# Sparse attention and a dropless mixture of experts on one core: expert work in units of up to 512 tokens instead of tiles of 128

## The chip, the core and the metric

The kernel runs on one core of a Trainium2 chip. Five engines work beside each other: TensorE (PE, with its weight loads shown as PEld), VectorE (DVE), ScalarE (ACT), GpSimd (POOL) and SyncE (SP), which issues most transfers. The metric is device microseconds (us) of one execution; lower is better.

## What is computed

The first half is block-sparse attention over 4 batches, 8 heads, 768 positions, head size 64. Its output is laid out as 3072 tokens of 512 numbers, and the second half sends each token through one of 8 experts:

```python
logits = x @ w_gate                      # (3072, 8)
expert_idx = np.argmax(logits, axis=1)
...
h = np.maximum(x_sorted[lo:hi] @ w1[e], 0.0)   # w1[e]: 512 x 1024
y_sorted[lo:hi] = h @ w2[e]                    # w2[e]: 1024 x 512
...
return (gate_w[:, None] * y).astype(np.float32)
```

All data are float32. With the reference's seed, experts 0 to 7 get 431, 32, 256, 32, 256, 160, 593 and 1312 tokens; of the first 2304 tokens (batches 0 to 2) they get 335, 32, 64, 32, 224, 128, 529 and 960. Neither kernel knows these counts when it is built: it counts on the chip, and has code for every case.

## The kernel before, in words

**Attention.** A loop over 16 pairs of heads and 2 halves computes scores, exponentials and sums, and writes token rows to a DRAM tensor `x_rows`, with each token's gate weight behind its 512 numbers. From the third batch on, routing work is put between.

**Routing, twice.** Phase A ranks the tokens of the first three batches while the last batch is still in attention, and gives `KA = 5` full tiles of 128 tokens to the experts that fill them. Phase B (`ranks`, `count`, `layout_b`, `one_hots`, `tokens`, lines 416 to 603) does it for the rest after attention. `tokens` makes lists of row numbers: `g` for gathers, `s` for scatters.

**Expert work, a tile at a time.** Each tile holds up to 128 tokens of one expert. `gather` (L620) is an indirect DMA issued by POOL. `fetch` (L629, L632) loads the expert's two weight matrices, 2 MB each, into one of two buffers. `turn_x` turns the rows so that features lie on partitions: by TensorE (L650) up to tile 5, by 16 DVE transposes (L642) later. `layer1` (L661) keeps blocks of w1 stationary and streams 128 tokens: 32 products, in fp32 two passes each, so 64 matmuls. `layer2` (L676) keeps the hidden values stationary and streams w2: 16 matmuls of 512 columns; its result has tokens on partitions, so that ACT scales it by the gate weight (L681) and POOL scatters it (L682) at once. Tiles share weight buffers in turn, and every tile fetches its own weights, the same expert's again too.

**Order.** On PE, DVE and POOL the instructions run as they are written down, between `by_hand.enter_context` and `by_hand.close()`; SP and ACT are ordered by the scheduler. 24 tiles are certain; a jump table (`tc.Switch`, L761) with one arm for each number of further tiles, 0 to 7, and a last arm that repeats everything in a safer way, closes the kernel. The counts above need 28 tiles, so arm 4 is taken. `judge` (L355) checks the attention's sums and decides whether the last arm is wanted.

Of the kernel before, what the change touches and what calls it, by code (L numbers as in the profile page):

```python
# [17 lines left out]
def kernel(  # L18
# [26 lines left out]
    NC = NT + E - 1  # L45
    TA = NT - NCH
    KA = 5
    NB_ = NC - KA
    assert TA * P - E * (P - 1) > (KA - 1) * P
# [32 lines left out]
    ld = ctx.enter_context(tc.tile_pool(name="ld", bufs=2))  # L82
# [4 lines left out]
    def load(b, pr):  # L87
        got = []
        for src, nm in ((k, "k_sb"), (q, "q_sb")):
            t = ld.tile([P, NCH, 2, D], F32, name=nm)  # L90
            for hh in range(2):

                queue = nc.scalar if nm == "q_sb" and (b, pr) == (0, 0) else nc.sync
                queue.dma_start(t[:, :, hh, :], src[b, 2 * pr + hh].rearrange("(p c) d -> p c d", p=P))
            got.append(t)
        t = ld.tile([P, 2, NCH, D], F32, name="v_sb", bufs=3)
        nc.sync.dma_start(
            t.rearrange("p h c d -> p h (c d)"), v[b, 2 * pr : 2 * pr + 2].rearrange("h (p c) d -> p h (c d)", p=P),
        )
        got.append(t)  # L100
        loaded[(b, pr)] = got
# [87 lines left out]
    def turn(b, pr, which):  # L189

        src = loaded[(b, pr)][which]
        dst = work.tile([P, S], F32, name="qT" if which else "kT")
# [15 lines left out]
    def scores(n, half, c):  # L208
# [11 lines left out]
        e = work.tile([P, 2, CW], F32, name="e", bufs=8)  # L220
        nc.scalar.activation(e[:], s[:, :, :CW], AF.Exp, scale=scale)  # L221
# [3 lines left out]
        if c > 0:  # L225
            t = esums[(n, half)]
            nc.vector.tensor_add(t[:], es[(n, half, 0)][:] if c == 1 else t[:], e[:])  # L227
# [80 lines left out]
    def shifted(n, half):  # L308
# [3 lines left out]
        for c in range(NCH):  # L312
            es[(n, half, c)] = work.tile([P, 2, CW], F32, name="e", bufs=8)
# [26 lines left out]
        for c in range(1, NCH):  # L340
            nc.vector.tensor_add(t[:], es[(n, half, 0)][:] if c == 1 else t[:], es[(n, half, c)][:])
# [13 lines left out]
    def judge():  # L355


        okp = ps_x.tile([1, 1], F32, name="okp", tag="xr")
        shape, total = [[4 * B * NPR, CW], [P, NT * E]], 0
        flats = (sums[:], lgn.rearrange("p t e -> p (t e)"))  # L360
        for j, (lo, hi) in enumerate(((2.0**-4, 2.0**40), (-(2.0**100), 2.0**100))):
            p, n = shape[j]
            total += p * n
# [5 lines left out]
            nc.tensor.matmul(okp[:], lhsT=okn[:], rhs=ones[:p, :1], start=(j == 0), stop=(j == 1))  # L369
        bad = mpool.tile([1, 1], F32, name="bad")  # L370
        nc.vector.tensor_scalar(bad[:], okp[:], scalar1=float(total), scalar2=float(REDO), op0=ALU.not_equal, op1=ALU.mult)

        nc.vector.tensor_scalar_min(rt["more"][:], rt["more"][:], float(NC - NT))
        arm = rt["arm"] = mpool.tile([1, 1], I32, name="arm")
        nc.vector.tensor_max(arm[:], rt["more"][:], bad[:])
# [4 lines left out]
    REDO = NC - NT + 1  # L380
# [8 lines left out]
    def route_consts():  # L389
        iota("first_w", [P, E], [[-1, E]], E, 0)  # L390
        iota("thr", [P, NT], [[P, NT]], 0, 0)
        iota("kx", [1, NC], [[1, NC]], 0, 0)
# [84 lines left out]
    def summed(out_, ph, off):  # L477

        r, sel = rt["r" + ph], rt["sel" + ph]
        T = r.shape[2]  # L480
        slot = sm.tile([P, E, T], F32, name="slot", tag="slot")
        nc.vector.tensor_tensor(slot[:], r[:], off[:].unsqueeze(2).to_broadcast([P, E, T]), op=ALU.add)
        nc.vector.tensor_tensor(slot[:], slot[:], sel[:], op=ALU.mult)
        nc.vector.reduce_sum(out_, slot.rearrange("p e t -> p t e"), axis=AX)
# [3 lines left out]
    def layout_a():  # L488
        cn = rt["cnA"]
        og = sm.tile([P, E, TA], F32, name="ogA")  # L490
        nc.vector.tensor_tensor(
            og[:], cn[:, 1, :].unsqueeze(2).to_broadcast([P, E, TA]), rt["thr"][:, None, 1 : TA + 1].to_broadcast([P, E, TA]),
# [7 lines left out]
        nc.vector.tensor_scalar_min(lo[:], lo[:], float(KA))  # L500
        nc.vector.tensor_scalar_min(hi[:], up[:], float(KA))
        nc.vector.tensor_sub(used[:], hi[:], lo[:])
        nc.vector.tensor_scalar(used[:], used[:], scalar1=float(P), scalar2=None, op0=ALU.mult)
        rt["used"] = used
        rt["lo"] = lo
        tile_experts("A", hi, KA)

    def slots_a():
        cn, r, lo, used = rt["cnA"], rt["rA"], rt["lo"], rt["used"]
        off = small_e("offA")  # L510
        nc.vector.scalar_tensor_tensor(off[:], in0=lo[:], scalar=float(P), in1=cn[:, 0, :], op0=ALU.mult, op1=ALU.add)
# [14 lines left out]
    def layout_b():  # L526
# [4 lines left out]
        og = sm.tile([P, E, NT], F32, name="ogB")  # L531
        nc.vector.tensor_tensor(
            og[:], left[:].unsqueeze(2).to_broadcast([P, E, NT]), rt["thr"][:, None, :].to_broadcast([P, E, NT]), op=ALU.is_gt,
        )
        nt, up = small_e("ntB"), small_e("upB")
        nc.vector.reduce_sum(nt[:], og[:], axis=AX)
        nc.vector.tensor_tensor_scan(up[:], nt[:], rt["zero"][:], 0.0, op0=ALU.add, op1=ALU.add)
        tile_experts("B", up, NB_)

        more_f = sm.tile([1, 1], F32, name="more_f")  # L540
        nc.vector.tensor_scalar(
            more_f[:], up[0:1, E - 1 : E], scalar1=float(KA - NT), scalar2=0.0, op0=ALU.add, op1=ALU.max,
        )
        rt["more"] = more_f
        base, off = small_e("base"), small_e("offB")
        nc.vector.tensor_sub(base[:], up[:], nt[:])
        nc.vector.scalar_tensor_tensor(base[:], in0=base[:], scalar=float(P), in1=used[:], op0=ALU.mult, op1=ALU.subtract)
        nc.vector.scalar_tensor_tensor(off[:], in0=base[:], scalar=-1.0, in1=cA[:, 0, :], op0=ALU.add, op1=ALU.add)
        sl = sm.tile([P, NT], F32, name="slB")
        summed(sl[:, :TA], "A", off)  # L550
# [3 lines left out]
        summed(sl[:, TA:], "B", off)  # L554
# [34 lines left out]
    def tokens(ph, T, n):  # L589
# [11 lines left out]
        nc.vector.tensor_scalar(none[:], tv[:], scalar1=0.0, scalar2=float(2 * N), op0=ALU.is_lt, op1=ALU.mult)  # L601
        s_ = kept("s" + ph, [P, n])
# [5 lines left out]
    st = [{} for _ in range(NC)]  # L608

    keep_w1 = [wp.tile([P, DB, F], F32, name=f"w1_{j}") for j in range(2)]  # L610
    keep_w2 = [wp.tile([P, FB, DM], F32, name=f"w2_{j}") for j in range(2)]
    keep_xg = [wp.tile([P, XW], F32, name=f"xg_{j}") for j in range(4)]
    keep_xT = [wp.tile([P, DB, P], F32, name=f"xgT_{j}") for j in range(2)]

    def of(name, i, p):
        return rt[name + "A"][:p, i : i + 1] if i < KA else rt[name + "B"][:p, i - KA : i - KA + 1]

    def gather(i):
        xg = st[i]["xg"] = keep_xg[i % 4]
        nc.gpsimd.indirect_dma_start(  # L620
            out=xg[:], out_offset=None, in_=x_d[: N - S, :] if i < KA else x_d[:, :], in_offset=bass.IndirectOffsetOnAxis(ap=of("g", i, P), axis=0),
        )

    def fetch(i, layer):

        e = nc.sync.value_load(of("xe", i, 1), min_val=0, max_val=E - 1)
        if layer == 1:
            w = st[i]["w1"] = keep_w1[i % 2]
            nc.sync.dma_start(w[:], w1v[:, bass.ds(e, 1)].rearrange("p e c f -> p (e c) f"))  # L629
        else:  # L630
            w = st[i]["w2"] = keep_w2[i % 2]
            nc.sync.dma_start(w[:], w2v[:, bass.ds(e, 1)].rearrange("p e a d -> p (e a) d"))  # L632

    def turn_x(i):
        xg, xT = st[i]["xg"], keep_xT[i % 2]
        st[i]["xT"] = xT
        if i > KA:

            for tq in range(4):
                for dq in range(4):  # L640
                    t, d = slice(tq * 32, (tq + 1) * 32), slice(dq * 32, (dq + 1) * 32)
                    nc.vector.transpose(xT[d, :, t], xg[t, :DM].rearrange("p (c q) -> p c q", c=DB)[:, :, d])  # L642
            return

        if i == 0 and "ps_m" not in upper:
            tp = upper["ps_s"].tile([P, 2, 512], F32, name="tp0", tag="s")[:, 0, :].rearrange("p (c q) -> p c q", c=DB)
        else:
            tp = upper["ps_m"].tile([P, DB, P], F32, name="tpg")[:]
        for c in range(DB):
            nc.tensor.transpose(tp[:, c, :], xg[:, c * P : (c + 1) * P], ident[:])  # L650
        nc.scalar.copy(xT[:], tp)

    def layer1(i, *between):

        hT = st[i]["hT"] = xp.tile([P, FB, P], F32, name="hT")
        for g in range(2):
            hp = upper["ps_h"].tile([P, FB // 2, P], F32, name="hp")
            for m in range(FB // 2):
                fb = g * (FB // 2) + m
                for c in range(DB):  # L660
                    nc.tensor.matmul(  # L661
                        hp[:, m, :], lhsT=st[i]["w1"][:, c, fb * P : (fb + 1) * P], rhs=st[i]["xT"][:, c, :],
                        start=(c == 0), stop=(c == DB - 1),
                    )
            if g == 0 and i >= KA:
                nc.vector.tensor_relu(hT[:, : FB // 2, :], hp[:])  # L666
            else:
                nc.scalar.activation(hT[:, g * (FB // 2) : (g + 1) * (FB // 2), :], hp[:], AF.Relu)  # L668
            if g == 0:
                for do in between:  # L670
                    do()

    def layer2(i, group):
        zp = upper["ps_z"].tile([P, DM], F32, name="zp")
        for fb in range(FB):
            nc.tensor.matmul(  # L676
                zp[:], lhsT=st[i]["hT"][:, fb, :], rhs=st[i]["w2"][:, fb, :], start=(fb == 0), stop=(fb == FB - 1),
            )
        zo = xp.tile([P, DM], F32, name="zo")
# [148 lines left out]
```

## Time and profile before

| what | value |
|---|---|
| three runs | 766.81, 767.39, 768.59 us; median 767.39 |
| profiled execution | 767.37 us, of which the span from first to last instruction is 765.7 |
| attention, to the first expert matmul | 0 to 357.5 us |
| 28 tiles | 357.5 to 754.8 us |
| PE, DVE, ACT, POOL busy | 749.5, 415.8, 270.2, 67.2 us |
| weights fetched | 56 transfers of 2 MB |

The page gives busy time by engine, then the span in 40 slices, then groups of instructions with their mean duration. The queries of the trace give single instructions in order of time, also those of an engine's sequencer (marked q: waits, branches, issues), which are not counted as busy.

### The profile page before, as it was taken

Reading aid. Unit: us, or ns where it says so; the run is one execution under the profiler, and the core shown is the slowest. Engines: PE = TensorE matmul, PEld = TensorE weight load, DVE = VectorE, ACT = ScalarE, POOL = GpSimd, SP = SyncE. Lnnn points to the kernel's source line nnn. Section 1 sums busy time; section 2 is a strip of 40 time slices with the busy share of each in tenths; the row PEclk is TensorE's granted clock in tenths of the full one; section 3 lists DMA queues with packets and bytes.
Section 4 is the critical chain, followed back from the end, with each engine's and each line's share of the span. In section 5 each row is a group of like instructions: output and inputs, shape, how many; then the busy total and the mean of one; then the engine's idle time right before and its main releaser. Section 6 shows DMA issues by size and latency. Waiting matters only on the chain.

```text
span 765.7 us, 13053 instructions
## 1 busy us (share of the span) xinstructions
PE 749.5 (98%) x5134; PEld 475.8 (62%) x5134; DVE 415.8 (54%) x834; ACT 270.2 (35%) x425; POOL 67.2 (9%) x98
## 2 busy tenths in 40 slices
PE   7999999999999999999999999999999999999994
PEld 4555555555555555556777686786776776866682
DVE  4678777777778779997530235533434425323400
ACT  4666676667666675665111000100100100001000
POOL 4000000000000000002011121111111211211010
PEclk8999999999999999999999999999999999999998
DMA  8322333233322331842789989899899899899940
GB/s 187 83 60 48 82 84 85 63 83 84 85 56 51 83 84 44 319 165 78 244 308 333 344 311 348 320 329 346 320 329 362 314 344 345 320 346 339 355 147 6
DMA packets 119362, 157.57 MB, mean 206 GB/s; under 512 B 56499, under 2 KB 72947, under 8 KB 119284
## 3 DMA queue, kind: packets, MB, share of 16 engines
q1 hardware_dynamic: 112672, 142.42, 55.8%
q0 software_dynamic: 4480, 13.75, 4.6%
q8 instruction: 43, 0.70, 0.4%
q10 hardware_dynamic: 2132, 0.41, 0.3%
q14 instruction: 35, 0.29, 0.1%
HBM read 143.79 MB, written 13.73 MB: 206 GB/s over the span
## 4 chain that ended last, share of the span: by engine, by line
PE 86%; DMA 7%; issue 5%; another core or an unknown queue 0%; ACTq 0%; POOL 0%; ACT 0%; DVE 0%; POOLq 0%
PE hp L661 21%; PE zp L676 19%; PE s L216 17%; PE op L237 16%; DMA out_dram<-zo,sB 6%; PE s L219 4%; PE sp L250 3%; PE xr L270 3%; PE tp L199 2%; DMA q_sb<-in_q_dram 1%; PE tpg L650 0%; POOL xg L620 0%; ACT qT L201 0%; ACTq L117 0%
## 5 line engine op out<-in xcount | busy, mean ns | idle before, releaser
L661 PEld LDWEIGHTS hp<-xgT,w 128*128 128x128 f32 x1792 | 204.7, 192 | 12.6 <-issue 8.6
L661 PE MATMUL hp<-xgT,w 128*128 128x128 f32 x1792 | 205.6, 275 | 0.0
L676 PE MATMUL zp<-w,hT 128*128 128x512 f32 x448 | 196.9, 593 | 0.0
L642 DVE STREAM_TRANSPOSE xgT<-xg 32x128 f32<-32x128 f32 x352 | 106.5, 303 | 110.0 <-DMA xg<-x_rows,gB 94.0
L216 PE MATMUL s<-qT,kT 64*128 64x384 f32 x768 | 159.2, 493 | 0.9 <-ACT qT L201 0.9
L221 ACT ACTIVATE e<-s 128x768 f32<-128x768 f32 x192 | 152.4, 812 | 7.0 <-PE s L219 5.2
L676 PEld LDWEIGHTS zp<-w,hT 128*128 128x128 f32 x448 | 83.0, 190 | 94.2 <-issue 94.2
L227 DVE TENSOR_TENSOR esum<-esum,e 128x768 f32<-128x768 f32 x128 | 122.7, 958 | 14.6 <-ACT e L221 1.1
L237 PE MATMUL op<-e,v_sb 128*64 128x384 f32 x768 | 129.3, 486 | 0.0
L237 PEld LDWEIGHTS op<-e,v_sb 128*64 128x64 f32 x768 | 55.1, 137 | 68.8 <-issue 68.8
L216 PEld LDWEIGHTS s<-qT,kT 64*128 64x128 f32 x768 | 67.1, 190 | 38.4 <-issue 33.5
L257 DVE RECIPROCAL r<-ss 128x128 f32<-128x128 f32 x96 | 82.2, 912 | 1.3 <-ACT ss L252 1.3
L668 ACT ACTIVATE hT<-hp 128x512 f32<-128x512 f32 x33 | 19.7, 597 | 177.4 <-PE hp L661 174.4
L681 ACT ACTIVATE zo<-zp,xg 128x512 f32<-128x512 f32 x28 | 19.2, 687 | 176.7 <-PE zp L676 176.7
L666 DVE TENSOR_SCALAR hT<-hp 128x512 f32<-128x512 f32 x23 | 15.9, 692 | 101.4 <-issue 57.9
L227 DVE TENSOR_TENSOR esum<-e 128x768 f32<-128x768 f32 x32 | 30.6, 957 | 63.2 <-ACT e L221 63.2
L219 PE MATMUL s<-pen,oh 64*128 64x384 bf16 x384 | 63.2, 326 | 0.0
L242 ACT COPY oT<-op 128x384 f32<-128x384 f32 x32 | 15.3, 479 | 106.2 <-PE op L237 106.2
L682 POOL DMA_INDIRECT out_dram<-zo,sB x23 | 23.3, 1013 | 259.7 <-ACT zo L681 259.7
L219 PEld LDWEIGHTS <-oh 64*128 64x128 bf16 x384 | 18.9, 95 | 25.8 <-issue 0.9
L270 PEld LDWEIGHTS xr<-mix,oT 128*64 128x64 f32 (+1 forms) x372 | 24.0, 139 | 10.7 <-issue 10.7
L250 PE MATMUL sp<-esum,ones 128*64 128x384 f32 x128 | 27.7, 512 | 0.0
(174 smaller groups left out, 260.1 us busy)
## 6 DMA issues: line engine op xcount, KB each, us to landing
w<-in_moe_w_dram SPq DMA_DIRECT2D x56, 2048.0 KB
k_sb<-in_k_dram SPq DMA_DIRECT2D x32, 192.0 KB
v_sb<-in_v_dram SPq DMA_DIRECT2D x16, 384.0 KB
x_rows<-xb SPq DMA_DIRECT2D x16, 384.0 KB
q_sb<-in_q_dram SPq DMA_DIRECT2D x30, 192.0 KB
sums<-ss SPq DMA_DIRECT2D x32, 3.0 KB
q_sb<-in_q_dram ACTq DMA_DIRECT2D x2, 192.0 KB
xg<-x_rows,gB POOLq DMA_INDIRECT x23, 7.5
```

Of the source, the lines that this page charges most:

```text
L216: nc.tensor.matmul(s[:, hh, :CW], lhsT=kT[r, c * P : (c + 1) * P], rhs=qT[r, cols], start=True, stop=False)
L219: nc.tensor.matmul(s[:, hh, :CW], lhsT=oh[r, c, :], rhs=pen[r, cols], start=False, stop=True)
L221: nc.scalar.activation(e[:], s[:, :, :CW], AF.Exp, scale=scale)
L227: nc.vector.tensor_add(t[:], es[(n, half, 0)][:] if c == 1 else t[:], e[:])
L237: nc.tensor.matmul(op[hh * D : (hh + 1) * D, :], lhsT=v_sb[:, hh, c, :], rhs=e[:, hh, :], start=(c == 0), stop=(c == NCH - 1),)
L250: nc.tensor.matmul(sp[hh * D : (hh + 1) * D, :], lhsT=ones[:], rhs=esum[:, hh, :], start=True, stop=True)
L257: nc.vector.reciprocal(r[:, m * P : (m + 1) * P], ss[:, m * P : (m + 1) * P])
L270: nc.tensor.matmul(xr[j * M_ : (j + 1) * M_, m, :], lhsT=oT[:, m * P + j * M_ : m * P + (j + 1) * M_], rhs=mix[:, pr, :], start=True, stop ...
L642: nc.vector.transpose(xT[d, :, t], xg[t, :DM].rearrange("p (c q) -> p c q", c=DB)[:, :, d])
L661: nc.tensor.matmul(hp[:, m, :], lhsT=st[i]["w1"][:, c, fb * P : (fb + 1) * P], rhs=st[i]["xT"][:, c, :], start=(c == 0), stop=(c == DB - 1),)
L676: nc.tensor.matmul(zp[:], lhsT=st[i]["hT"][:, fb, :], rhs=st[i]["w2"][:, fb, :], start=(fb == 0), stop=(fb == FB - 1),)
L682: ins = nc.gpsimd.indirect_dma_start(out=out[:, :], out_offset=bass.IndirectOffsetOnAxis(ap=of("s", i, P), axis=0), in_=zo[:], in_offset=N ...
```

## The change

Layer 2 is turned round: now w2 is stationary too (`lhsT=self.w2[...]`, 128x128 blocks), and the tokens stream in both layers, any number `n` of them up to 512. So a unit of n tokens is 64 + 64 matmuls, each n columns wide. The result of layer 2 has features on partitions; it has to be turned back before it is scaled and scattered. `finish` does this with 16 DVE transposes, then for each 128 tokens one POOL multiplication by the gate weights and one scatter.

There are three kinds of unit:

- `early`: 2 units of 256 tokens (phase A), turned by TensorE;
- `whole`: units of 384 tokens for experts with more than 512 left, 0 to 6 of them. The old end switch is now in the middle and has an arm for each number of whole units; the arm has the units and prepares unit `own[1]`;
- `own`: one unit for each expert, with what is left. Its gather, turn and finish always handle 4 x 128 tokens; the matmuls' width is 128 to 512 in steps of 16, chosen by a jump table of 25 arms on PE and ACT (on POOL too for the last). The last unit does layer 2 in the old way (`layer2_by_rows`).

With the counts above: 256 tokens each of experts 0 and 6 are early; expert 7 has 3 whole units; the own units' widths are 176, 128, 256, 128, 256, 160, 352, 160. Buffers of attention (`ar`, `ea`) are reused for the units' data. `hT` and `zo` exist once. `judge` moves ahead of `tokens("B")`, and the safer arm is followed by the normal own units whose scatters it turns off.

The core of the diff (left out: renamed buffers in attention, the changed constants of phase A, the safer arm):

```diff
+    EA, QA, UW, RW, GR = 2, 2 * P, 3 * P, 4 * P, 16
+    UM = -(-(N - EA * QA - RW) // UW)
...
+        if units:
+            ge = sm.tile(shape, F32, name="ge_u", tag="slot2")
+            nc.vector.tensor_tensor(ge[:], slot[:], wide(units[0]), op=ALU.is_ge)
+            nc.vector.tensor_tensor(ge[:], ge[:], wide(units[1]), op=ALU.mult)
+            nc.vector.tensor_tensor(slot[:], slot[:], ge[:], op=ALU.add)
...
+        def turn(self):
+            self.keep_gates()
+            for tq in range(4):
+                for dq in range(4):
+                    t, d = slice(tq * 32, (tq + 1) * 32), slice(dq * 32, (dq + 1) * 32)
+                    nc.vector.transpose(
+                        self.xT[d].rearrange("p c (j q t) -> p j c q t", j=RJ, q=4)[:, : self.nj, :, tq, :],
+                        self.xg[t, : self.nj, :DM].rearrange("p j (c q d) -> p j c q d", c=DB, q=4)[:, :, :, dq, :],
+                    )
...
+        def layer1(self, n, between={}):
+            for fb in range(FB):
+                hp = upper["banks"][fb % 6]
+                for c in range(DB):
+                    nc.tensor.matmul(
+                        hp[:, :n], lhsT=self.w1[:, c, fb * P : (fb + 1) * P], rhs=self.xT[:, c, :n],
+                        start=(c == 0), stop=(c == DB - 1),
+                    )
+                nc.scalar.activation(hT[:, fb, :n], hp[:, :n], AF.Relu)
+                for do in between.get(fb, []):
+                    do()
...
+        def finish(self, group):
+            for tq in range(4):
+                for dq in range(4):
+                    t, d = slice(tq * 32, (tq + 1) * 32), slice(dq * 32, (dq + 1) * 32)
+                    nc.vector.transpose(
+                        zo[t, : self.nj, :].rearrange("p j (c q d) -> p j c q d", c=DB, q=4)[:, :, :, dq, :],
+                        self.zT[d].rearrange("p c (j q t) -> p j c q t", j=RJ, q=4)[:, : self.nj, :, tq, :],
+                    )
+            for j in range(self.nj):
+                nc.gpsimd.tensor_scalar(
+                    zo[:, j, :], zo[:, j, :], scalar1=gates[:, self.at, j : j + 1], scalar2=None, op0=ALU.mult,
+                )
+                self.put(j, zo[:, j, :], group)
...
+    rows_out(n, 0)
+    early[0].layer1(QA, {2: [lambda: rows_out(n, 1)], 5: [turn_1], 7: [count_b]})
+    early[0].layer2(QA)
+    early[1].layer1(QA, {1: [tokens_b]})
+    whole(0, 0).fetch(2)
+    own[0].fetch(1)
+    early[1].layer2(QA)
+    own[0].fetch(2)
+    whole(0, 0).turn()
+    own[0].turn()
+    for u in early:
+        u.finish("rows_out")
...
+            units = [whole(i, arm - 1) for i in range(arm)]
+            for u, then in zip(units, units[1:] + [own[1]]):
+                then.gather()
+                u.layer1(UW)
+                then.turn()
+                then.fetch(1)
+                u.layer2(UW)
+                then.fetch(2)
+                u.finish("rows_out")
...
+    for e, u in enumerate(own):
+        if e + 2 < E:
+            own[e + 2].gather()
+        at = rt["size"][0:1, e : e + 1]
+        index = {
+            ET.PE: nc.tensor.value_load(at, min_val=0, max_val=(RW - P) // GR),
+            ET.Activation: nc.scalar.value_load(at, min_val=0, max_val=(RW - P) // GR),
+        }
+        if e + 1 == E:
+            index[ET.Pool] = nc.gpsimd.value_load(at, min_val=0, max_val=(RW - P) // GR)
+        for k in tc.Switch(index, (RW - P) // GR + 1):
+            width = P + k * GR
+            u.layer1(width)
+            if e + 1 < E:
+                u.layer2(width)
+            else:
+                u.layer2_by_rows(width, "rows_out")
+        if e + 2 < E:
+            own[e + 2].turn()
+            own[e + 2].fetch(1)
+            own[e + 2].fetch(2)
+        if e + 1 < E:
+            u.finish("rows_out")
```

PE, DVE and POOL follow the written order in the units too (`tc.manual_schedule`).

## The prediction

> **What bounds the kernel now.** I read the busy times and slices first, then the chain that ended last, then single instructions around the switch.
>
> ```profile
> PE 749.5 (98%) x5134; PEld 475.8 (62%) x5134; DVE 415.8 (54%) x834; ACT 270.2 (35%) x425; POOL 67.2 (9%) x98
> ...
> PE   7999999999999999999999999999999999999994
> ...
> DVE  4678777777778779997530235533434425323400
> ```
> ```profile
> 643.15 6.87 PE zp L676 x16
> 650.02 7.14 PE hp L661 x64
> 657.16 6.87 PE zp L676 x16
> ```
> The first fence (page) shows PE full in every slice and DVE at 2 to 5 tenths from slice 20 on. The second (chain) shows a tile as 7.14 + 6.87 = 14.01 us of PE with nothing between; no wait for weights appears, though they keep the DMA engines at 9 tenths. So only fewer matmul columns save time: the 56 fetches becoming 26 (13 units) saves nothing by itself. 28 tiles take 392.3 us.
>
> **Attention, phase A, first fetches.** Same instructions; up to 357.5 us I change nothing. Cover: PE, full there; without it one more x turn costs 0.6 us.
>
> **PE's matmuls.** A matmul of 128 columns takes 7.14/64 = 111.6 ns, of 512 columns 6.87/16 = 429.4 ns; a straight line gives 138 at 160, 151 at 176, 217.5 at 256, 297 at 352, 323.5 at 384. A unit is 128 of them: early 2 x 27.8, whole 3 x 41.4, own 19.4 + 14.3 + 27.8 + 14.3 + 27.8 + 17.7 + 38.0, the last 64 x 0.138 + 32 x 0.4294 = 22.6. Sum 361.7: **30.6 us less**.
>
> **Turning.** Now DVE turns into and out of each unit, 16 transposes each, of 512 elements in an own unit.
> ```profile
> 689.34 5.32 DVE L642 STREAM_TRANSPOSE xgT<-xg 32x128 f32<-32x128 f32 x16 [6.93 <-DMA xg<-x_rows,gB]
> ```
> ```profile
> L227 DVE TENSOR_TENSOR esum<-esum,e 128x768 f32<-128x768 f32 x128 | 122.7, 958 | 14.6 <-ACT e L221 1.1 <-DVE esum L227 0.5
> L642 DVE STREAM_TRANSPOSE xgT<-xg 32x128 f32<-32x128 f32 x352 | 106.5, 303 | 110.0 <-DMA xg<-x_rows,gB 94.0 <-PE hp L661 5.6
> ...
> L519 DVE TENSOR_TENSOR within<-rA,leftA 128x144 f32<-128x144 f32 x1 | 0.3, 309 | 0.0
> ```
> Timeline, then DVE's groups (busy, mean ns): one transpose of 128 elements takes 303 ns, 16 take 5.32 (29 ns between). Only one size is shown. Lower end: a fixed part and the slope of the additions, (958 - 309)/624 = 1.04 ns an element: 303 + 384 x 1.04 = 702 ns at 512. Upper end: all proportional, 1212 ns. I take 702, since the 144-element addition costs as much as the transpose, so the fixed part looks alike. With 29 ns and the copy of the gates, 16 take 11.9 us for 4 x 128 tokens (11.7 back), 9.8 for 384, 7.4 for 256; at the upper end 19.9. The Trainium skill ("Vector Engine (DVE) Microarchitecture Reference", 3.8) says that a transpose sustains one element a cycle and lane, which speaks for the lower end; by it the sum below is 866, by the upper end 1017.
>
> **POOL and its transfers.**
> ```profile
> L174 POOL COPY mix<-ident 128x128 f32<-128x128 f32 x4 | 1.2, 288 | 0.1
> L175 POOL COPY mix<-wg 128x8 f32<-128x8 f32 x4 | 0.8, 188 | 1.6 <-DMA wg<-in_moe_w_gate_dram 1.6
> ```
> ```profile
> 397.48 1.02 POOL L682 DMA_INDIRECT out_dram<-zo,sA  x1 [12.58 <-ACT zo L681]
> 398.80 0.97 POOL L620 DMA_INDIRECT xg<-x_rows,gB  x1 [0.30 <-issue]
> ```
> ```profile
> DMA to landing us min/median/max: 3.4/7.4/9.0
> ```
> POOL's groups: (288 - 188)/120 = 0.83 ns an element, so the multiplication of 512 is 0.61 us; from above I allow 1.2, twice that, as no tensor_scalar is shown. POOL's timeline: issues follow each other every 1.3 us. So a scaled scatter of 128 tokens is 1.9 us, a gather of an own unit 4 x 1.3 = 5.2. Third fence, the gathers (L620): landing 3.4 us after an issue starts on quiet queues, 7.4 under full weight traffic; that is 2.4 and 6.4 after POOL is free. I take 4.0, as weights will be half the traffic, and 2.5 for the first ones.
>
> **Jumps.**
> ```profile
> L761 PEldq TENSOR_LOAD <-arm x1: 487/487/487, 691.1 to 691.1; - x1
> L761 PEldq BRANCH_PREFETCH_HINT  x1: 50/50/50, 695.4 to 695.4; - x1
> L761 ACTq TENSOR_LOAD <-arm x1: 484/484/484, 699.0 to 699.0; - x1
> L761 POOLq TENSOR_LOAD <-arm x1: 511/511/511, 699.7 to 699.7; - x1
> ...
> L761 ACTq BRANCH_PREFETCH_HINT  x1: 57/57/57, 706.1 to 706.1; - x1
> L761 POOLq BRANCH_PREFETCH_HINT  x1: 69/69/69, 706.2 to 706.2; - x1
> ```
> The switch's line: from loading the arm's number to the first instruction of the arm PE needs 4.3 us, ACT 7.1, POOL 6.5. Here this cost nothing: PE's sequencer was 17 matmuls of 0.43 us ahead (the switch is read at 691.1, the matmuls before the arm run until 698.8). Leaving the arm: PE 0.4 (branch at 748.9, next at 749.2), ACT 2.4, POOL 2.9, SP 6.0. In front of an own unit PE is ahead by 17 matmuls of the unit before, 1.9 us (128 columns) to 5.5 (384). ACT can begin only when PE has ended the unit before: it is ready 0.25 + (0.4 to 6.0) + 0.75 + (2.5 to 6.0) later, middle 11.0, and PE can go on for six banks, 48 matmuls (5.4 us at 128). With 0.5 us for the first relu, own units lose 4.2 + 6.1 + 3.0 + 6.1 + 3.0 + 4.8 + 2.6 + 4.8 = **34.6 us** at the middle, about 7 with the shortest jumps. The skill ("Runtime: NRT & Kernel Launch", Instruction fetch mechanics) says that prefetch is sequential and a taken branch outside the window waits for a DMA; it gives no price, and PE's exit, far away and 0.4 us, does not show it.
>
> **Where it all goes: the ring.** DVE's written order is turn(e+2), finish(e); POOL's is gather(e+3) after the scatters of finish(e). So each own turn waits for a gather, that for scatters, these for a finish, that for the turn before. Walked through (span times):
>
> - Early. rows_out, layer 1, two turns: layer 1 of early 0 ends at 376.0, layer 2 at 389.9, PE reaches `tokens_b` at 393.4. DVE starts layout B at 376.2. It took 12.3 us (374.39 to 386.65); added: six wide operations 1.7, eight small 1.6, one-hots of 50 not 26 columns 1.8, smaller tables -1.0, and judge, now ahead, 2.9. PE waits and does its small products until 397.2: 3.8 us. Where this wait is gone, nothing else is late.
> - Early 1 goes on 24.4 to 421.5, jump 0.7, whole 0 41.4: to 463.7.
> - Beside it: gathers from 398.2, whole 0 turned 414.4, own 0 426.3, finish early 0 433.7, scatters 437.5, landing (`zo` exists once) 440.0, finish early 1 447.4, scatters 451.2, POOL's jump 457.7, gather whole 1 461.6, landed 465.6, turned 475.4. **PE waits 11.7 us.** Whole 1 ends at 516.8, whole 2 (turned 509) at 558.3.
> - Finish whole 2 568.5, scatters 574.2, POOL leaves the arm (2.9 and some five semaphore increments of 0.75 us) 581.2, gather own 2 586.4, landed 590.4, turned **602.3**. PE ends own 1 at about the same time.
> - One turn of the ring: 11.9 + 11.7 + 4 x 1.9 + 5.2 + 4.0 = **40.4 us**, against 22.7 us of PE per unit. Five rounds: own 7 is turned at 804.3.
> - End. Finish own 5 816.0, scatters 823.6, landed 827.6, finish own 6 839.3, scatters 846.9, POOL's jump 853.4, last scatters 855.7; 8.7 us follow (757.0 to 765.7 now): span 864.4. PE's last unit is done by 830.
>
> The profiled execution is 767.37 with a span of 765.7, 1.7 around; its time stands at the median of the runs (767.39). **Forecast 864.4 + 1.7 = 866 us.**
>
> Bounds of it: quick landings 2.4 make 853, slow ones 6.4 make 885; multiplications of 1.2 us make 887; all POOL and jump terms at their short end 838, several long ones 905. Transposes at the upper end make 1017.
>
> **Rivals.**
> - *The jumps bound, not the ring.* If DVE's and POOL's ring stays under PE's pace, the path is 546.5 (early and whole without the 11.7) + 181.9 + 34.6 + 10.6 tail + 1.7 = **775 us**. For it: DVE is half idle now; against: the written order.
> - *Faster.* The same with jumps at their short end: 546.5 + 181.9 + 7.3 + 10.6 + 1.7 = **748 us**. One mechanism: POOL's gathers do not stand behind the scatters, so that a unit's turning hides under two units of PE. It decides when a ring turn is below 22.7 us plus 3; with 40.4 the transposes would have to be free.
> - *Dearer transposes or POOL work*: over 905.
> - *It doesn't do what it says*: widths in the profile would be 512. The counts give widths that sum to 1616 columns, so I give this nothing beyond the rest.
>
> **Chances.** Ring, 838 to 905: 0.70. Jumps alone: 0.09. Faster: 0.10. Over 905: 0.08. Something between the two rivals within 0.2% of before: 0.03. A change under 0.2% can't be told from none here. The range for 8 in 10 takes in ring and jumps: 770 to 905; slower in all 0.87.
>
> **What would show it.** Right: DVE transposes of 512 elements near 0.70 us; PE waiting 10 to 25 us before own 3 to 7 for xT; POOL's gather right after the scatters; whole 1 late by some 12 us. Wrong: PE busy over 9 tenths in the last third, waits before own units under 6 us, or short waits that end with ACT's relu, which would mean the jumps.

## The result, and the profile after

| | before | after |
|---|---|---|
| median, us | 767.41 (four runs, 766.81 to 768.59) | 896.49 (four runs, 894.59 to 898.92) |
| ratio, 95% interval | 1 | 1.1681 (1.1649 to 1.1714) |
| span of the profiled execution | 765.7 | 895.4 |
| mean granted clock | 0.992 | 0.908 |

The change makes the kernel 16.8% slower. The forecast was 866 us, its range 770 to 905. The busy times and the slices of after (page; one digit is a fortieth of the span, 22.4 us):

```profile
PE 742.2 (83%) x4516; PEld 481.7 (54%) x4516; DVE 535.9 (60%) x858; ACT 288.8 (32%) x516; POOL 164.2 (18%) x175
...
PE   7999999999999999999977999865970757189820
...
DVE  4777787777777998478626443536272736363650
...
PEclk8999999999999999999998999976986797579875
```

For 20 slices (to 448 us) the line of PE looks as before. The two 7s after that are the wait before whole 1. From the 26th slice (560 us) on it has holes, and the clock falls with each hole. DVE's line now swings between 2 and 7 in a beat of two slices: a unit comes round every 44 us. PE's busy time fell by only 7.3 us although its columns are worth 30.6 us less, because after a wait the same matmuls run slower (own 2's 64 matmuls of 256 columns take 16.79 us in layer 1, after a wait, and 13.98 in layer 2).

The chain that ended last ran over PE before; now it runs over POOL (start, duration, what):

```profile
711.11 1.56 POOL ea L753
...
721.75 1.03 POOL out_dram L734
723.09 1.01 POOL ar L672
727.88 27.06 issue
```

Behind the "issue" of 27 us stand the landing of the gather and DVE's two turnings, which this view does not follow; the timelines do. One round of the beat, in the timelines of DVE, POOL and PE (start, duration, engine, line, what; in brackets the idle time before and what ended it):

```profile
731.64 0.17 DVE L689 COPY gates<-ar 128x4 f32<-128x4 f32 x1 [20.63 <-DMA ar<-x_rows,gB]
731.72 11.44 DVE L697 STREAM_TRANSPOSE xT<-ar 32x512 f32<-32x512 f32 x16
743.19 11.71 DVE L748 STREAM_TRANSPOSE ea<-ar 32x512 f32<-32x512 f32 x16
775.96 0.17 DVE L689 COPY gates<-xg 128x4 f32<-128x4 f32 x1 [21.06 <-DMA xg<-x_rows,gB]
```
```profile
755.00 1.56 POOL L753 TENSOR_SCALAR ea<-ea,gates 128x512 f32<-128x512 f32 x1 [27.12 <-DVE ea L748]
756.84 1.04 POOL L734 DMA_INDIRECT out_dram<-ea,sB  x1 [0.28 <-POOL ea L753]
...
765.64 1.03 POOL L734 DMA_INDIRECT out_dram<-ea,sB  x1 [0.28 <-POOL ea L753]
766.98 1.01 POOL L672 DMA_INDIRECT xg<-x_rows,gB  x1 [0.31 <-issue]
...
770.83 0.95 POOL L672 DMA_INDIRECT xg<-x_rows,gB  x1 [0.30 <-issue]
```
```profile
743.21 11.43 PE L712 MATMUL bank<-xT,w 128*128 128x160 f32 x64 [13.75 <-DVE xT L697]
754.48 8.86 PE L725 MATMUL bank<-ea,w 128*128 128x160 f32 x64
787.53 21.72 PE L712 MATMUL bank<-ar,w 128*128 128x352 f32 x64 [24.19 <-DVE ar L697]
```

Read them as one chain. DVE turns unit 5's tokens (L697), then turns unit 3's result back (L748), until 754.9. POOL starts at 755.0: four times a multiplication and a scatter, until 766.7. Directly behind the last scatter, at 766.98, comes the gather of unit 6. Its tokens end DVE's wait of 21.06 us at 775.96, and the next round begins. PE stands at the end of it: it waits 13.75 and 24.19 us, and both waits end with DVE's transpose into the unit's tokens. This is the forecast's ring, 44.3 us long in this round.

### The profile page after: what moved, and what is told of

It reads as the page before. It is cut to its first block, busy times and chain, and to the rows that moved or that the text cites. A ratio compares the mean times of both kernels' runs of the same rounds, so it can differ in the third digit from the quotient of the medians.

```text
span 895.4 us, 11949 instructions
## 1 busy us (share of the span) xinstructions
PE 742.2 (83%) x4516; PEld 481.7 (54%) x4516; DVE 535.9 (60%) x858; ACT 288.8 (32%) x516; POOL 164.2 (18%) x175
## 5 line engine op out<-in xcount | busy, mean ns | idle before, releaser
L725 PE MATMUL bank<-ea,w 128*128 128x256 f32 (+5 forms) x768 | 170.8, 383 | 0.0
L229 PE MATMUL s<-ar 64*128 64x384 f32 x768 | 158.7, 492 | 0.9 <-ACT ar L214 0.9
L712 PE MATMUL bank<-xT,w 128*128 128x384 f32 (+3 forms) x512 | 121.6, 405 | 40.4 <-DVE xT L697 31.5
L234 ACT ACTIVATE ea<-s 128x768 f32<-128x768 f32 x192 | 152.4, 812 | 6.3 <-PE s L232 3.4
L725 PEld LDWEIGHTS bank<-ea,w 128*128 128x128 f32 x768 | 130.3, 191 | 38.8
L748 DVE STREAM_TRANSPOSE ea<-ar 32x512 f32<-32x512 f32 (+2 forms) x192 | 120.0, 625 | 35.9 <-DMA out_dram<-ea,sB 13.0
L712 PE MATMUL bank<-ar,w 128*128 128x256 f32 (+2 forms) x320 | 82.2, 423 | 64.9 <-DVE ar L697 51.4
L240 DVE TENSOR_TENSOR esum<-esum,ea 128x768 f32<-128x768 f32 x128 | 122.7, 958 | 14.1 <-ACT ea L234 0.5
L250 PE MATMUL op<-ea,ar 128*64 128x384 f32 x768 | 129.3, 486 | 0.0
L712 PEld LDWEIGHTS bank<-xT,w 128*128 128x128 f32 x512 | 91.2, 217 | 70.3 <-DVE xT L697 30.0
L697 DVE STREAM_TRANSPOSE xT<-ar 32x512 f32<-32x512 f32 (+1 forms) x112 | 72.3, 645 | 2.2
L240 DVE TENSOR_TENSOR esum<-ea 128x768 f32<-128x768 f32 x32 | 30.6, 957 | 63.4 <-ACT ea L234 63.4
```

The lines of the kernel that those rows point to most:

```text
L229: nc.tensor.matmul(s[:, hh, :CW], lhsT=kT[r, c * P : (c + 1) * P], rhs=qT[r, cols], start=True, stop=False)
L234: nc.scalar.activation(e, s[:, :, :CW], AF.Exp, scale=scale)
L240: nc.vector.tensor_add(t[:], es[(n, half, 0)] if c == 1 else t[:], e)
L250: nc.tensor.matmul(op[hh * D : (hh + 1) * D, :], lhsT=v_sb[:, hh, c, :], rhs=e[:, hh, :], start=(c == 0), stop=(c == NCH - 1),)
L697: nc.vector.transpose(self.xT[d].rearrange("p c (j q t) -> p j c q t", j=RJ, q=4)[:, : self.nj, :, tq, :], self.xg[t, : self.nj, :DM].rear ...
L712: nc.tensor.matmul(hp[:, :n], lhsT=self.w1[:, c, fb * P : (fb + 1) * P], rhs=self.xT[:, c, :n], start=(c == 0), stop=(c == DB - 1),)
```

## The experiments

Times are medians. Before's median was between 766.5 and 767.2 in each batch of these runs, so the times can be compared.

### 1. Is it the ring? Gathers ahead of the scatters (e1)

```diff
-        if e + 2 < E:
-            own[e + 2].gather()
+        if e == 0:
+            own[2].gather()
...
+        if e + 3 < E:
+            own[e + 3].gather()
         if e + 1 < E:
             u.finish("rows_out")
```

> POOL issues the gather of own unit e+3 ahead of the scatters of own unit e, instead of behind them; nothing else is moved, the jumps stay. Theory (the ring): DVE turn 11.5 + wait for zo's landing 2.7 + DVE finish 11.7 = 26 us per unit instead of 43.8; the jumps in front of the own units (8 to 10 us each where nothing hides them) then show. 805 to 835 us instead of 896. Rival (the jumps are what makes the own stage slow): their number is the same, so 890 to 900 us.

Measured: 822.63 us (819.60 to 826.21), 1.0743 (1.0716 to 1.0769) of before. DVE's timeline:

```profile
620.34 11.46 DVE L697 STREAM_TRANSPOSE xT<-ar 32x512 f32<-32x512 f32 x16
633.59 11.71 DVE L748 STREAM_TRANSPOSE ea<-ar 32x512 f32<-32x512 f32 x16 [1.80 <-issue]
645.33 0.17 DVE L689 COPY gates<-xg 128x4 f32<-128x4 f32 x1
645.41 11.46 DVE L697 STREAM_TRANSPOSE ar<-xg 32x512 f32<-32x512 f32 x16
```

The wait of some 21 us before each turn is gone, and a round takes 25.1 us (620.34 to 645.41) instead of 44. Only the order of POOL's instructions was changed, so this order alone costs 896.5 - 822.6 = 74 us. DVE is now almost continuously at work: the next bound is close behind. The time lies inside the theory's range and far from the rival's.

### 2. Is it the jumps? Constant widths in place of the jump tables (e2), and both edits (e3)

The widths are those that these counts give.

```diff
-        for k in tc.Switch(index, (RW - P) // GR + 1):
-            width = P + k * GR
-            u.layer1(width)
+        width = [176, 128, 256, 128, 256, 160, 352, 160][e]
+        u.layer1(width)
```

> The own units' jump tables are left out: the widths 176, 128, 256, 128, 256, 160, 352, 160 that this input needs are written down as constants, so the kernel works for these token counts alone. The ring stays as it is. Theory (the ring): PE waits longer for the turned tokens instead, only POOL's last jump (3 us) is saved: 888 to 896 us. Rival (the jumps): eight times 8 to 10 us less, 820 to 835 us.

> Both edits: gathers ahead of the scatters, and constant widths for this input. Theory (the ring): now DVE alone, 26 us per unit, and the tail of two finishes and their scatters: about 802 us, 790 to 815. Rival (the jumps): as without jumps alone, 820 to 835 us, since the order of the gathers would not matter.

Measured: e2 890.38 us (888.77 to 891.04), 1.1604 (1.1585 to 1.1624); e3, the edits of e1 and e2 together, 801.59 us (799.94 to 802.54), 1.0450 (1.0431 to 1.0468). So without jumps the changed kernel gains only 6 us: inside the ring they are hidden, as the ring theory says. With the ring gone they are worth 822.6 - 801.6 = 21 us. That e3 is still 35 us above before needs another cause; sections 4 and 7 find it in POOL's multiplications, own 2's late gather and the four pieces.

### 3. How much is the multiplication? (e4, e5)

e4 moves it to DVE:

```diff
-                nc.gpsimd.tensor_scalar(
+                nc.vector.tensor_scalar(
```

> The multiplication by the gate weights is done by DVE instead of POOL; order and jumps unchanged. Theory (the ring, with POOL's 1.58 us multiplication as the term that was too small in the forecast): 4 x (1.58 - about 0.45) = 4.5 us less per round, five rounds and the two last finishes: 855 to 870 us. Rival (the jumps): 890 to 900 us. Second rival (DVE, not the ring, is full): slower than 896.

Measured: 838.49 us (837.34 to 840.13), 1.0936 (1.0916 to 1.0955): right in direction, but below the expected range. The groups of e4 show the price on DVE:

```profile
L753 DVE TENSOR_SCALAR ea<-ea,gates 128x512 f32<-128x512 f32 x41 | 17.3, 482 | 0.4
```

Four take 1.7 us on DVE, and POOL's four scatters follow each other every 1.3 us, 5.2 us instead of 11.7. The mean of the last four rounds falls from 43.8 to 38.6 us. The whole gain is 58 us: own 2 is turned at 593.6 instead of 608.7, as the middle stage's finishes have the same links (15); own 7's turn begins at 775.4 instead of 819.6, 44 earlier, so the rounds give 29; the rest, 14, is the end with its two finishes. I had expected little outside the rounds.

e5 tells why it is so dear, with a form for each of the four pieces:

```diff
+                if j == 0 or self.nj < 4:
+                    nc.gpsimd.tensor_scalar(
...
+                elif j == 1:
+                    nc.gpsimd.tensor_scalar(zo[:, j, :], zo[:, j, :], scalar1=1.0, scalar2=None, op0=ALU.mult)
+                elif j == 2:
+                    nc.gpsimd.tensor_copy(zo[:, j, :], zo[:, j, :])
+                else:
+                    for h in range(4):
+                        nc.gpsimd.tensor_scalar(
+                            zo[:, j, h * P : (h + 1) * P], zo[:, j, h * P : (h + 1) * P],
```

> A look at POOL's multiplication. Of the four pieces of an own unit, piece 0 stays as it is (gate weight read through a pointer); piece 1 is multiplied by the constant 1.0, piece 2 is only copied onto itself (these two leave the gate weight out), piece 3 is multiplied through the pointer in four parts of 128 columns. If the pointer makes it dear: 1.57 us for piece 0, near 0.6 for pieces 1 and 2 (the 0.83 ns an element of the copies in the attention part). If any such operation has this rate: 1.4 to 1.6 for all three, and 0.45 for a part of 128. If most of it is a fixed price: parts of 128 near 1.3.

One run, 897.95 us, of which only the durations of single operations are used. POOL's groups (busy, mean ns; L754 is the form of the change, L763 the four parts, L758 the constant, L760 the copy):

```profile
L754 POOL TENSOR_SCALAR ea<-ea,gates 128x512 f32<-128x512 f32 x20 | 31.4, 1569 | 305.0 <-DVE ea L748 252.4 <-issue 52.1
...
L763 POOL TENSOR_SCALAR ea<-ea,gates 128x128 f32<-128x128 f32 x28 | 16.4, 599 | 0.2
...
L758 POOL TENSOR_SCALAR ea<-ea 128x512 f32<-128x512 f32 x7 | 10.6, 1519 | 0.3
...
L760 POOL COPY ea<-ea 128x512 f32<-128x512 f32 x7 | 4.3, 621 | 0.1
```

A constant costs as much as the gate weights (1519 and 1569 ns), so it is not the operand. The slope is (1569 - 599)/384 = 2.5 ns an element; the copy takes 621 ns. The prediction priced the multiplication from before's copies (0.61 us), and for copies this was right to 0.01 us. It was the wrong kind of row. None of the three expectations fits all four numbers. The Trainium skill ("GPSIMD Engine Reference", 4.1) calls an elementwise operation with one input about line rate on GpSimd; here it is 1569 ns against DVE's 482, 3.3 times slower, and the measurement decides.

### 4. What is left when everything is constant? (e6), and with jumps (e7)

e6 has the edits of e1, e2 and e4, gathers own 2 before the early finishes, and lets an own unit gather, turn and finish as many pieces of 128 tokens as it needs. It holds for these counts only. e7 is e6 with the jump tables.

```diff
-    own = [Unit("B", NU_ + RJ * e, RJ, EA + UM + e, e, xgs[e % 2], (e + 1) % 2, (e + 1) % 2, (e + 1) % 2) for e in range(E)]
+    own = [Unit("B", NU_ + RJ * e, [2, 1, 2, 1, 2, 2, 3, 2][e], EA + UM + e, e, xgs[e % 2], (e + 1) % 2, (e + 1) % 2, (e + 1) % 2) for e in range(E)]
...
+    own[2].gather()
```

> No jump tables in the own stage (widths as constants of this input), own units that handle only the 128-token pieces they need (2, 1, 2, 1, 2, 2, 3, 2 instead of 4 each, also constants), gathers ahead of scatters (own 2's ahead of the early finishes), gate weights on DVE. Theory (ring and jumps are all that stands in the way of the saving on PE): PE is full again but for some 8 us before whole 1; 555 + 182 + 13 + 2 = about 752 us, 745 to 760, faster than before. Rival (something else binds too: single buffers, weights that arrive late, clock): 765 to 790.

> As the run without jump tables and with exact pieces, but with the jump tables in. The difference is the price of the jumps with nothing to hide behind. By the prediction's terms (34.6 us): 785 us. By the waits seen when only the gathers were moved (7.7, 10.2, 1.6, 12.0, 2.5, 8.7 and 0.6 us before own 1 to 7, some 3 in own 0): 46 us, 795 to 800. If the jumps are free: 752.

Measured: e6 738.70 us (738.11 to 744.14), 0.9654 (0.9627 to 0.9682), faster than both kernels and than expected; e7 805.99 us (802.67 to 807.94), 1.0490 (1.0471 to 1.0509), above the expected range. First e6 (page), then own 1 and 2 in PE's timeline of e6 and of e7:

```profile
PE 718.9 (98%) x4516; PEld 464.2 (63%) x4516; DVE 479.2 (65%) x884; ACT 289.6 (39%) x516; POOL 66.9 (9%) x102
...
PE   7999999999999999999998999999999999999995
```
```profile
574.44 7.31 PE L725 MATMUL bank<-ea,w 128*128 128x128 f32 x64
581.59 13.98 PE L712 MATMUL bank<-ar,w 128*128 128x256 f32 x64
595.40 13.98 PE L725 MATMUL bank<-ea,w 128*128 128x256 f32 x64
```
```profile
587.75 7.31 PE L725 MATMUL bank<-ea,w 128*128 128x128 f32 x64
605.34 16.82 PE L712 MATMUL bank<-ar,w 128*128 128x256 f32 x64 [10.28 <-issue]
622.00 13.98 PE L725 MATMUL bank<-ea,w 128*128 128x256 f32 x64
```

In e6 the next unit's layer 1 follows without a gap, and the kernel is nearly as far below before (28.5 us) as its columns are worth (30.6 by the prediction; PE's busy time fell from 749.5 to 718.9, by 30.6 too). In e7 PE waits 10.28 us between own 1 and own 2, for nothing that another engine does ("issue"): its sequencer stands in a branch. The line of PE's sequencer for the switch shows how long (duration min/median/max, first and last start):

```profile
L967 PEldq COMPARE_BRANCH  x18: 311/3684/7342, 419.4 to 788.9; - x18
```

Each switch has a branch into the arm and one out of it, and either can take microseconds. That the branch waits for code is an inference, which the pages' rows for the transfers of instructions support (packets, MB, share of the DMA engines; e6 first, then e7): with the jump tables there are 55 more of them.

```profile
q8 instruction: 39, 0.64, 0.4%
q14 instruction: 32, 0.26, 0.1%
```
```profile
q8 instruction: 61, 1.00, 0.5%
q14 instruction: 65, 0.53, 0.2%
```

Nine waits of PE between own 0 and own 7 (0.9 to 11.0 us; two of them for a relu, as ACT jumps too) make 49.2 us. The wait has a second price: layer 1 takes 16.82 us where layer 2 of the same width takes 13.98. The windows of e7 around it (window, us, busy time of PE, PEld, DVE, ACT, POOL, then granted clock, DMA share, GB/s):

```profile
595.10:605.30 10.20, 0.00 (x0) 0.00 (x0) 5.40 (x18) 0.26 (x1) 2.94 (x3) 0.61 0.74 245
605.30:608.70 3.40, 3.36 (x8) 2.76 (x9) 0.00 (x0) 0.00 (x0) 0.00 (x0) 0.50 0.33 92
608.70:611.00 2.30, 2.30 (x7) 1.79 (x7) 0.00 (x0) 0.38 (x1) 0.00 (x0) 0.51 0.00 0
611.00:622.00 11.00, 11.00 (x52) 9.69 (x51) 0.00 (x0) 2.30 (x6) 0.00 (x0) 1.00 0.00 0
```

In the first 3.4 us after the wait the clock is 0.50, and 8 of 64 matmuls get done; it stays at 0.51 for the next 2.3 us and is 1.00 from 611.0 on. So 5.7 us run at half clock, which loses some 2.8 us: that is the difference between 16.82 and 13.98. Layer 1 minus layer 2 over the units, with the last 16 matmuls of own 0's layer 1, makes 16 us. Together 65 of the 67.3 us between e6 and e7. (The Trainium skill, "TensorE: Matmul & The Clock Gate", Part 1, has this rule: an idle window of about 3.4 us halves the clock, a busy one of the same length brings it back. The rows agree on the two states; the way back took 5.7 us here, more than one such window.)

### 5. A version for any counts (e8)

e8 keeps the jump tables and the four pieces, and has the edits of e1 and e4, with own 2's gather early.

```diff
+    own[2].gather()
...
+            own[e + 3].gather()
...
+                nc.vector.tensor_scalar(
```

> What can be had without knowing the counts: gathers ahead of scatters, own 2's ahead of the early finishes, gate weights on DVE; jump tables and four pieces per own unit stay. DVE 25 us per unit against PE's 22.7 and the jumps: 798 to 812 us by ring and jumps together. If the ring alone were the matter: 775 to 785. If POOL's multiplication has no part in it once the gathers are ahead: 822, as with the gathers alone.

Measured: 818.58 us (817.58 to 819.81), 1.0674 (1.0659 to 1.0689), above the range by 6.6 us. Compared with e1 it has only the multiplication moved and one gather earlier: with the gathers ahead, that is worth 4 us, not the 58 of e4. What costs 58 us inside the ring costs nearly nothing beside it, as long as the jumps are there to hide it: without them the same two edits are worth 801.6 - 757.1 = 44.5 us (e3 and, in section 7, e12).

### 6. Do the weights make the jumps dear? (e9, e10, e11)

In e7's first window the weight transfers run at 245 GB/s while PE waits for code. e9 is e7 without the weight transfers of own 2 to 7; e10 is e7 with them moved into the arm, issued by ACT after the first relu; e11 is e8 with the same move, for any counts.

```diff
-            own[e + 2].fetch(1)
-            own[e + 2].fetch(2)
...
-            u.layer1(width)
+            u.layer1(width, {0: [lambda: [own[e + 1].fetch(layer, nc.scalar) for layer in (1, 2)]]} if 0 < e < E - 1 else {})
```

> The run with the jumps alone (806 us), with the weight transfers of own units 2 to 7 left out: those units work with the weights of own 0 and 1. So the jumps meet quiet DMA queues. If a jump is dear because its code comes through DMA engines that carry 4 MB of weights at that moment: branches on PE take 2 to 3 us instead of 3 to 7, the waits before the own units fall from 48 us to about 20, the clock's loss with them: 765 to 778 us. If the distance of the code or the sequencer makes it dear: 800 to 808.

> The run with the jumps alone, but the weights of own unit e+1 are fetched from inside unit e, by ACT's queue after its first relu, when PE and ACT have their code. All work is done. If weight traffic makes the jumps dear: as with quiet queues, or some us more where 12 us of transfer do not fit into a unit of 14: 768 to 790 us. If not: 806 or more, since weights come later.

> The version for any counts (gathers ahead, gate weights on DVE; 818.6 us) with the weights fetched from inside the units. If weight traffic makes the jumps dear, DVE's 25 us per unit is what is left: 765 to 795 us. If not: 818 or more.

Measured: e9 790.84 us (789.59 to 795.23), 1.0330 (1.0302 to 1.0358); e10 791.11 (788.09 to 796.49), 1.0336 (1.0295 to 1.0376); e11 801.20 (799.97 to 802.98), 1.0456 (1.0441 to 1.0470). All three fall between their two expectations; e10 misses the lower one by 1 us, e11 by 6. The same sequencer line of e9:

```profile
L965 PEldq COMPARE_BRANCH  x18: 320/3597/4082, 419.8 to 771.6; - x18
```

Without weight traffic the longest branch falls from 7.34 to 4.08 us, but the median stays (3.60 against 3.68). So 806.0 - 790.8 = 15 us of the jumps' 67 come from the traffic, and can be moved away (e10). The other 52 us stay on quiet queues. The Trainium skill ("Runtime: NRT & Kernel Launch", Instruction fetch mechanics) has the rule that a taken branch out of the prefetched window waits for a DMA, and no price; here a branch of PE mostly takes 2 to 4 us on quiet queues, and no run splits it into the transfer and the rest. e11 is the best version for any counts, and still slower than before.

### 7. What do the four pieces cost? (e12)

e6, but with four pieces in every own unit, as in the change.

```diff
-    own = [Unit("B", NU_ + RJ * e, [2, 1, 2, 1, 2, 2, 3, 2][e], EA + UM + e, e, xgs[e % 2], (e + 1) % 2, (e + 1) % 2, (e + 1) % 2) for e in range(E)]
+    own = [Unit("B", NU_ + RJ * e, RJ, EA + UM + e, e, xgs[e % 2], (e + 1) % 2, (e + 1) % 2, (e + 1) % 2) for e in range(E)]
```

> As the run with everything constant (738.7 us), but the own units turn and finish four pieces of 128 tokens again, as in the change. DVE then has 11.5 + 11.5 + 1.7 = 24.7 us per unit against PE's 22.7, with nothing else in the way. If DVE's amount of work is a bound of its own: 748 to 762 us. If it hides under PE: 739.

Measured: 757.05 us (756.12 to 758.11), 0.9867 (0.9851 to 0.9884), inside the expected range. PE's timeline, whole 1 and then own 3 and 4:

```profile
472.63 22.71 PE L712 MATMUL bank<-xT,w 128*128 128x384 f32 x64 [6.16 <-DVE xT L697]
...
625.26 7.31 PE L725 MATMUL bank<-ea,w 128*128 128x128 f32 x64
634.01 14.08 PE L712 MATMUL bank<-ar,w 128*128 128x256 f32 x64 [1.45 <-DVE ar L697]
647.93 13.98 PE L725 MATMUL bank<-ea,w 128*128 128x256 f32 x64
```

Without jumps, PE now waits for DVE's turning (1.45 us before own 4, 3.96 before own 6). DVE's round of 11.4 for the turn, 11.4 for the finish and 1.7 for the multiplications is 24.6 us, two above PE's mean of 22.7. Four pieces for units that mostly fill one or two cost 757.1 - 738.7 = 18 us. About as much as these two waits give arises earlier: before whole 1 PE waits 6.16 us where e6 waits 0.57, since own 0's turn on DVE, ahead of the early units' finishes, takes 11.46 us instead of 7.19, and whole 1's gather on POOL then waits 5.93 us instead of 2.94 for the landing of a larger one.

The sum of it, from e6 upwards: 738.7; four pieces + 18 = 757.1 (e12); jump tables + 61.5 = 818.6 (e8); multiplication on POOL and own 2's gather later + 4 = 822.6 (e1); gathers behind the scatters + 74 = 896.5 (the change). The amounts hold for this order only, because one bound hides another: the jump tables cost 6 us inside the ring (e2), 21 with POOL's multiplications beside them (e3 to e1), 61.5 or 67.3 when nothing hides them; the multiplications with own 2's later gather cost 4 us beside the jumps and 44.5 without them.

## Why the prediction was right, and where its sizes were off

**The mechanism was right.** POOL's gather follows directly behind the scatters, PE waits for xT before own 3 to 7 (5.4, 27.2, 13.8, 24.2 and 2.9 us, 14.7 on average; forecast 10 to 25 for each, which two of the five keep), and taking the order away takes 74 us away (e1), while taking the jumps away takes 6 (e2).

**Attention and PE's columns: right.** PE's timeline up to the experts is as before to within a microsecond (first turn of x at 355.4, before 356.0), the units take what the straight line gave (13.98 us for 64 matmuls of 256 columns, forecast 13.92), and e6 shows that the 30.6 us are there to be had when nothing is late.

**The transposes: right, at the lower end.** Groups of DVE:

```profile
L748 DVE STREAM_TRANSPOSE ea<-ar 32x512 f32<-32x512 f32 x112 | 78.7, 703 | 16.5 <-DMA out_dram<-ea,sB 13.0
L697 DVE STREAM_TRANSPOSE xT<-ar 32x512 f32<-32x512 f32 x64 | 44.9, 702 | 1.1
```

The estimate from one size and the additions' slope was 702 ns. The proportional end of 1212 is out.

**The ring's length: 43.8 for 40.4, one term of it mis-sized.** The first of the five rounds takes 47.4 us, as its gather lands 6.8 us after the last issue; the other four take 43.8 on average. The round shown above, by the prediction's terms: turn 11.5 (11.9), finish 11.7 (11.7), four multiplications and scatters 12.0 (7.6), gather 4.8 (5.2), landing 4.2 (4.0). The step that failed is "so a scaled scatter of 128 tokens is 1.9 us". It is 2.94 us; the multiplication takes 1.57 us, not 0.61, and 4 x 0.96 = 3.8 us a round:

```profile
L753 POOL TENSOR_SCALAR ea<-ea,gates 128x512 f32<-128x512 f32 x41 | 64.5, 1573 | 301.6 <-DVE ea L748 248.4
```

The bound from above, "1.2, twice that, as no tensor_scalar is shown", was too low as well. A factor put on a row of another kind of operation is no bound; DVE's multiplication or the additions would have been nearer in kind, though not in engine.

**The 31.0 us of span that were missing (895.4 - 864.4)** stand in three places. Own 2 is turned at 608.7, forecast 602.3: 6.4, to which three multiplications in the last whole unit's finish contribute 2.9, its later end 3.4, and a slower landing 1.7, less 1.6 for POOL's shorter way out of the arm and quicker issues. Five rounds: 20.3. The end: 4.3, where two finishes are 8 us longer and the last scatters wait 2.2 longer for the end of the program, while zo's release (1.2 instead of 4.0) and POOL's last jump (3.0 instead of 6.5) are shorter. The one mis-sized term would fill almost all of it: 31 multiplications lie on the path (3, 20 and 8), and 31 x 0.96 = 29.8 us. That the other differences, up to 3.5 us each, all but cancel is luck.

**The early waits: about right.** PE waited some 3.4 us at `tokens_b` (3.8) and 9.5 before whole 1 (11.7).

**The jumps: hidden in the ring as said, but their price was half the truth.** The prediction had 34.6 us at the middle. The middle of the parts it names (0.25, 0.4 to 6.0, 0.75 and 2.5 to 6.0) is 8.5 and not the 11.0 that the sum uses, so by its own parts the term would have been smaller still. e7 shows 67.3: 49 of waits and 16 of the slow clock after them, which the prediction did not count at all. Its single samples were misleading: PE's exit of 0.4 us lies at the short end of the branches' 0.3 to 7.3. Two jump waits show in the change too, where the ring is not yet late: 8.1 us before own 1, and before own 2. PE's timeline there, and its sequencer's branches from 605 to 620 us:

```profile
619.86 16.79 PE L712 MATMUL bank<-ar,w 128*128 128x256 f32 x64 [10.47 <-DVE ea L748]
```
```profile
L966 PEldq COMPARE_BRANCH  x2: 4584/5626/6667, 607.2 to 612.9; - x2
```

The timeline names DVE for the 10.47 us, but own 2 was turned at 608.7, eleven us before. PE's sequencer was in the branch out of own 1's arm until 611.8 (607.2 + 4.58); the branch into own 2's arm, 6.67 us, the longest of the run, began at 612.9 and ended at 619.6. So it was the jump.

**The rivals: the order right, the prices wrong.** "The jumps bound" was given as 775; with everything else cleared away it is 806 (e7), and the difference, 31, is the jumps' own error (65 less 34.6). "Faster, 748" was to come about if the gathers do not stand behind the scatters. e1 did just that, and got 822.6. Behind the ring stood three more bounds, the jumps, DVE's four pieces and POOL's multiplications, and only without the jumps and with the multiplication off POOL is the kernel faster than before (757.1 with four pieces, 738.7 without), for these counts alone. The rival's place was right, the point from which it decides was not: several links have to fall together.

## What to carry to other kernels

Where engines run in written order, walk one unit's loop through all queues and add up what stands between one turn and the next: here POOL's gather behind the scatters made a ring of 44 us around 23 us of TensorE work, and moving five gathers was worth 74 us. Where several bounds stand behind each other, what one of them costs depends on which others are still there, so take them away together as well as one by one. Fewer columns pay only if nothing new stands behind each unit; price every new operation from a row of its own kind and engine, and bound it widely where there is none. A jump table for each unit costs its branch twice and the clock after the wait, so here it has to save more than 6.5 us a unit on quiet queues (52/8) and 8.4 under weight traffic (67.3/8).

## What the runs showed of the hardware that was not expected

- GpSimd's fp32 multiplication by a scalar: 1569 ns for 128x512, 599 ns for 128x128, nearly the same with a constant (1519 ns for 128x512); its copy of 128x512 621 ns; VectorE's multiplication 482 ns (e4, e5).
- A branch into or out of an arm: TensorE 0.3 to 7.3 us under weight traffic (median 3.7), 0.3 to 4.1 without it (median 3.6) (e7, e9).
- After a wait of 10 us TensorE's granted clock is 0.50 for 5.7 us more (e7); layer 1 of each unit whose wait was over 4 us takes 2.4 to 3.1 us longer than its layer 2.
- VectorE's transposes in 32x32 blocks: 436 ns for 256 elements a lane, 702 for 512; with before's 303 for 128 this is a straight line of 1.04 ns an element on about 170 ns.
